# A fused attention and SoLU kernel: the second parts of its weights made by products with unit matrices, its chunks taken from two batches by turns, all steps in a new order

## The chip, the cores and the metric

The kernel runs on one core of one Trainium2 chip. The metric is device time in microseconds, the median of three runs. One execution was also recorded by the hardware profiler; times of single instructions are from that one.

## The reference

Attention over 4 batches, 8 heads, 768 positions and a head size of 64, in which a query sees the first `n_sink` keys and a window of the last `window` ones; then, per token, two matrix products with an exponential and a normalisation between them.

```python
scores = scale * np.matmul(q, k.transpose(0, 1, 3, 2))
keep = is_sink | in_window                     # n_sink = 4, window = 128
scores = np.where(keep, scores, -1000000000.0)
a = softmax(scores); attn_out = np.matmul(a, v)
x = attn_out.transpose(0, 2, 1, 3).reshape(3072, 512)
h = x @ w_in                                   # 512 x 1024, held as 64-bit floats
solu = h * softmax(h)
ln = (solu - mean) / np.sqrt(var + 1e-06) * g_ln
out = ln @ w_out                               # 1024 x 512, held as 64-bit floats
```

## The kernel before

The 3072 tokens are 24 chunks of 128 (`n`), six to a batch (`NC`). A chunk needs its own 128 keys, the 128 before them in its batch, and the sinks. Every large product is made in two parts: a tile is split into its value rounded to the matmul type (`xh`, `w1h`, `w2h`, `uh`) and the rest (`xl`, `w1l`, `w2l`, `ul`), and three products with fp32r operands stand for one exact one.

One chunk goes through these steps, each a small function:

- `load_*` bring q, k and v; `turn_q`, `turn_k` transpose them on TensorE (L486); `take_*` and `rest_*` split them (L511, L517, L534, L539); keys go to a ring of four slots (`ring`), with the sinks copied beside each (`ring_sinks`); `swap_q` swaps halves of the queries by DMA (`qX`).
- `score` (L565, L566) makes 128 x 264 scores per head, `pick` and `mask` (L572, L583) choose and mask, `exps` (L593), `invert` and `normalise` (L604 on GpSimd) finish the softmax.
- `turn_p` (L611), `p_hi`, `p_lo` (L621) and `part_new`, `part_old` (GpSimd) make the transposed weights in two parts; `value` (L680 to L685) multiplies with this chunk's and the last chunk's values (`vs`) and the sinks' (`vsink`, L471 to L477); `gather` (L693), `shift` (DMA `ysh`) and `tokens` give `xt`; `x_hi`, `x_lo` split it.
- `hidden` (L731) makes `h`, 24 products of 512 columns into the only `h` buffer (two PSUM banks); `highest` and `peak` (L738, L743: `mx`, `nm`) wait for it; `solu_exp`, `solu` (L748, L753), `centre`, `square`; `turn_u` (L785), `u_hi`, `u_lo` (L789, L793); `project` (L800), 24 products into `o`; `scale`, `store`.

Chunk 0 is "native": its scores (L563) and values (L673) are plain fp32 products without splitting, since nothing else uses TensorE yet.

The weights come as 64-bit floats in 16 blocks of 128 x 512: blocks 0 to 7 are `w_in`, 8 to 15 are `w_out`. For each block, ScalarE takes the magnitude of the high words (`size_w`, L389), VectorE clamps it (`least_w`, L396), shifts it into the place of an fp32 number (`move_w`, L400), puts the sign in (`sign_w`, L404) and the top bits of the low words (`rest_w`, L409). `gain_w` (L416, ScalarE) multiplies `w_out` blocks by `g_ln`; `w_hi` (L423, ScalarE) rounds; `w_lo` (L428) subtracts, on VectorE for blocks 1, 3, 5 and 7 and on GpSimd for the others.

Each engine runs its instructions in the order of the program, which is set by hand: `PLAN`, `PLAN_W`, `FIRST` and `OWN` give every step of every chunk and block a number, and the steps are called in the order of these numbers. The numbers are sort keys, not times.

Of the kernel before, what the change touches and what calls it, by code (L numbers as in the profile page):

```python
# [10 lines left out]
F32 = mybir.dt.float32  # L11
# [9 lines left out]
    "load_k": (-47.23,),  # L21
    "load_q": (-49.03,),
    "load_v": (-40.42,),
    "turn_q": (-40.51,),
    "turn_k": (-37.07,),
    "take_q": (-40.3, -40.3),
    "rest_q": (-38.64, -38.21),
    "swap_q": (-37.8, -35.74),
    "keep_k": (-2.79,),
    "take_k": (-36.17, -35.65),  # L30
    "rest_k": (-34.67, -34.63),
    "ring_sinks": (-37.2,),
# [12 lines left out]
    "sinks_lo": (-17.35, -15.21),
    "v_hi": (-29.23, -19.54),
    "v_lo": (-19.05, -9.81),
    "sink_values": (-2.64,),
    "turn_sinks": (-13.45,),
    "take_sinks": (-11.96,),  # L50
    "value": (-7.08, -10.1, -4.27, -1.3),
    "gather": (-5.52, -8.67, -2.61, 0.37),
    "shift": (-3.46, 2.91),
    "tokens": (-1.59, 5.21),
    "x_hi": (-0.2, 5.51),
    "x_lo": (-0.09, 8.07),
    "hidden": (5.97, 7.49, 10.82, 12.58, 7.4, 10.94, 11.18, 12.62),
    "highest": (15.14, 15.95),
    "peak": (16.22,),
    "solu_exp": (17.91,),  # L60
    "solu": (19.52,),
    "centre": (21.83,),
    "square": (29.39,),
    "variance": (32.89,),
# [935 lines left out]
```

## Time and profile before

| | before |
|---|---|
| median of 3 runs | 529.26 us (528.01 to 530.07) |
| the profiled execution, whole | 532.71 us |
| its span, first to last instruction | 530.9 us |
| mean granted TensorE clock | 0.983 |
| ScalarE, GpSimd busy | 355.0 us (67%), 325.8 us (61%) |
| HBM read, written | 27.53 MB, 6.42 MB |

PE is TensorE's matmul, PEld its weight load, DVE is VectorE, ACT ScalarE, POOL GpSimd, SP the engine that issues all DMAs. A matmul row's own duration holds its way through the array; what a stream of them costs is the distance from one start to the next. A row of a group reads: line, engine, operation, output<-inputs, shapes, count, busy time in us, mean ns of one, and the idle time of the engine before them with what ended it.

### The profile page before, as it was taken

The numbers are of one execution on the slowest core, as the hardware profiler recorded it, in microseconds if no ns is written. First come the engines' busy times: TensorE is split into PE (matmuls) and PEld (weight loads), VectorE is DVE, ScalarE is ACT, GpSimd is POOL, SyncE is SP. The second block draws the span as 40 slices with busy tenths as digits, with TensorE's granted clock in tenths as the row PEclk, the third lists the DMA queues.
The fourth block names the chain that finished last, engine by engine and source line by source line (L and its number), as shares of the span: only waits on it lengthen the run. The fifth ranks groups of instructions, "written<-read, shape, count | busy, mean of one in ns | idle before, by whom it ended". The sixth has DMA issues, their size and how long they took to land.

```text
span 530.9 us, 9053 instructions
## 1 busy us (share of the span) xinstructions
PE 464.2 (87%) x2572; PEld 385.8 (73%) x2572; DVE 421.1 (79%) x1238; ACT 355.0 (67%) x945; POOL 325.8 (61%) x445
## 2 busy tenths in 40 slices
PE   0242776999989999999999999999999999999995
PEld 0131565878877888888888788787888878888874
DVE  3999879899968679888878997888789888777531
ACT  3674747768876476776776768577778767666442
POOL 1276427798864267677764658667854766677620
PEclk9999977899999999999999999999999999999999
DMA  6974332543532514533533543462654332320101
GB/s 239 303 163 99 99 62 51 108 102 79 137 86 61 128 31 120 130 71 104 113 87 78 120 103 74 103 156 52 135 138 94 75 93 70 79 73 15 56 31 44
DMA packets 103303, 52.57 MB, mean 99 GB/s; under 512 B 80400, under 2 KB 92176, under 8 KB 103248
## 3 DMA queue, kind: packets, MB, share of 16 engines
q1 hardware_dynamic: 103248, 51.93, 39.4%
q8 instruction: 23, 0.38, 0.3%
q14 instruction: 32, 0.26, 0.2%
HBM read 27.53 MB, written 6.42 MB: 64 GB/s over the span
## 4 chain that ended last, share of the span: by engine, by line
PE 60%; DVE 25%; DMA 4%; issue 4%; ACT 3%; POOL 3%; SPq 0%; DVEq 0%; POOLq 0%; ACTq 0%
PE o L800 18%; PE h L731 18%; PE s L565 4%; PE s L566 3%; DMA ysh<-y 3%; PE av L680 3%; PE utp L785 3%; DVE ring L539 3%; PE av L683 3%; PE ptp L611 2%; DVE qT L517 2%; DVE y L693 2%; DVE wbits L409 2%; DVE s L572 2%; DVE wbits L404 2%
## 5 line engine op out<-in xcount | busy, mean ns | idle before, releaser
L604 POOL TENSOR_TENSOR sc<-sc,rs 128x544 f32<-128x544 f32 (+1 forms) x48 | 52.7, 1097 | 76.1 <-DVE rs L599 64.0
L731 PE MATMUL h<-w1h,xh 128*128 128x512 f32 x192 | 82.3, 429 | 0.3 <-DVE u L753 0.3
L593 ACT ACTIVATE sc<-sc,nmx 128x136 f32<-128x136 f32 (+1 forms) x192 | 76.3, 401 | 8.1 <-DVE nmx L583 7.7
L800 PE MATMUL o<-w2h,uh 128*128 128x512 f32 x192 | 79.6, 415 | 0.0
L731 PE MATMUL h<-w1h,xl 128*128 128x512 f32 x192 | 76.7, 400 | 1.4 <-POOL xl L720 1.4
L565 PE MATMUL s<-ring,qT 128*128 128x264 f32 (+1 forms) x184 | 59.9, 327 | 19.6 <-DVE ring L539 9.5
L800 PE MATMUL o<-w2h,ul 128*128 128x512 f32 x192 | 76.3, 397 | 0.0
L731 PE MATMUL h<-w1l,xh 128*128 128x512 f32 x192 | 76.3, 397 | 0.0
L800 PE MATMUL o<-w2l,uh 128*128 128x512 f32 x192 | 75.7, 394 | 0.0
L693 DVE TENSOR_REDUCE y<-av 128x256 f32<-128x512 f32 x92 | 63.1, 687 | 9.6 <-POOL xl L720 5.2
L583 DVE CUSTOM_DVE_ANT_0 sc<-s,bias 128x136 f32<-128x136 f32 (+1 forms) x192 | 55.5, 295 | 13.4 <-PE s L566 6.9
L565 PEld LDWEIGHTS s<-ring,qT 128*128 128x128 f32 x184 | 36.9, 200 | 34.6 <-issue 15.4
L628 POOL TENSOR_SCALAR_AFFINE_SELECT pc<-pt 128x1024 fp32r<-128x1024 f32 x40 | 43.8, 1095 | 24.4 <-DVE pt L621 21.6
L566 PE MATMUL s<-ring,qX 128*128 128x264 f32 (+1 forms) x184 | 54.8, 300 | 1.7 <-DMA qX<-qT 1.7
L710 POOL TENSOR_TENSOR xt<-y,ysh 64x256 f32<-64x256 f32 x46 | 33.5, 729 | 35.7 <-DMA ysh<-y 29.7
L680 PE MATMUL av<-pc,vs 128*128 128x256 f32 x160 | 43.6, 294 | 3.3 <-DVE y L693 2.7
L793 DVE TENSOR_TENSOR ul<-utp,uh 128x512 fp32r<-128x512 f32 x48 | 33.0, 688 | 16.8 <-ACT uh L789 15.9
L731 PEld LDWEIGHTS h<-w1h,xl 128*128 128x128 f32 x192 | 36.6, 190 | 10.3 <-POOL xl L720 1.8
L634 POOL TENSOR_SCALAR_AFFINE_SELECT pt<-pt 128x1024 fp32r<-128x1024 f32 x40 | 43.7, 1092 | 0.4
L715 ACT CAST xh<-xt 128x256 fp32r<-128x256 f32 x46 | 18.7, 406 | 37.4 <-POOL xt L711 37.1
L800 PEld LDWEIGHTS o<-w2h,ul 128*128 128x128 f32 x192 | 36.1, 188 | 10.5 <-DVE ul L793 2.0
L683 PE MATMUL av<-pt,vs 128*128 128x256 f32 x160 | 42.4, 287 | 0.0
(132 smaller groups left out, 1294.2 us busy)
## 6 DMA issues: line engine op xcount, KB each, us to landing
qX<-qT SPq DMA_DIRECT2D x92, 128.0 KB, 2.3
kn<-in_k_dram SPq DMA_DIRECT2D x24, 256.0 KB, 4.0
qn<-in_q_dram SPq DMA_DIRECT2D x24, 256.0 KB, 3.6
vn<-in_v_dram SPq DMA_DIRECT2D x24, 256.0 KB, 3.2
out_dram<-ob SPq DMA_DIRECT2D x24, 256.0 KB, 2.4
ysh<-y SPq DMA_DIRECT2D x92, 64.0 KB, 2.1
wraw<-in_moe_w_in_dram SPq DMA_DIRECT2D x8, 512.0 KB, 6.9
wraw<-in_moe_w_out_dram SPq DMA_DIRECT2D x8, 512.0 KB, 6.4
```

Of the source, the lines that this page charges most:

```text
L565: nc.tensor.matmul(o, st["qT", n, x][:, r, :], rhs, start=True, stop=False)
L566: nc.tensor.matmul(o, st["qX", n, x][:, r, :], rhs, start=False, stop=True)
L583: nc.vector.tensor_tensor_reduce(out=st["sc", n, hb][:, j, c0:c1], in0=st["s", n, h].rearrange("p a x -> p (a x)")[:, c0:c1], in1=bias0 if ...
L593: nc.scalar.activation(sc[:, i, c0:c1], sc[:, i, c0:c1], AF.Exp, bias=nmx[:, i:i + 1], scale=-1.0, accum_out=ssum[:, i:i + 1])
L604: nc.gpsimd.tensor_tensor(sc[:, :, c0:c1], sc[:, :, c0:c1], rs.unsqueeze(2).to_broadcast([P, HB, c1 - c0]), op=ALU.mult)
L628: nc.gpsimd.affine_select(pc, pt.bitcast(F32), pattern=[[0, HB * 2], [1, P]], compare_op=ALU.is_ge, fill=0.0, base=0, channel_multiplier=-1)
L634: nc.gpsimd.affine_select(pt, pt.bitcast(F32), pattern=[[0, HB * 2], [-1, P]], compare_op=ALU.is_ge, fill=0.0, base=-1, channel_multiplier=1)
L680: nc.tensor.matmul(acc[:, x], lhs, pc[:, 2 * jp + x], start=(x == 0), stop=(alone and x == 1))
L683: nc.tensor.matmul(acc[:, x], lhs, pt[:, 2 * jp + x], start=False, stop=False)
L693: nc.vector.tensor_reduce(st["y", n, hb][:, jp], st["acc", n, pr].rearrange("p x s q -> p x q s"), axis=AX.X, op=ALU.add)
L731: nc.tensor.matmul(st["h", n][:, cols], a[:, kt % 2, :], w[:, kt, cols], start=(kt == 0 and m == 0), stop=(kt == KT1 - 1 and m == 2))
L800: nc.tensor.matmul(st["o", n], a[:, kt % 4, :], part(w, kt), start=(kt == 0 and m == 0), stop=(kt == KT2 - 1 and m == 2))
```

## The change

It has four parts.

1. **The weights' words.** `size_w` and `least_w` go. `lower_w` (ScalarE) scales the high words, read as fp32, by 2 to the -112, which puts the exponent where the shift needs it and keeps the sign; the masks of `move_w` and `sign_w` change with it, their number does not.
2. **The second parts.** `w_lo` is no subtraction any more. For each block, TensorE multiplies the fp32 block with a 128 x 128 diagonal of minus one (`dg_8`) or of minus `g_ln` (`dg_0` to `dg_7`, made by `gains`), in fp32, into PSUM (`sum_w`); adds the rounded part through the unit matrix in fp32r (`less_w`); and ScalarE takes the result out with the sign turned (`w_lo`). `w_in` blocks use the `h` buffer in PSUM for that, `w_out` blocks one of the two `tr` buffers that the transposes `ptp` and `utp` use. `gain_w` goes: `w_hi` multiplies by `g_ln` as it rounds. The diagonals take the two buffers of `xt`; `dg_8` keeps one until the last `w_in` block, so the others follow each other through the second.
3. **Two batches by turns.** `place` makes chunk n the chunk of batch 0 or 1 (later 2 or 3) by its parity, so that a chunk's predecessor is n - 2. Chunks 0 and 1 are both the first of a batch, and both are native. Each batch has two slots of the ring of its own, so the sinks are copied for the first two chunks of a batch only. `vs` has 8 buffers for 5, `vsink` and `vsraw` 2 for 1.
4. **The order.** All four tables of sort keys are new.

```diff
-    "load_k": (-47.23,),
...
+    "load_k": (-39.8,),
...
-    def size_w(_, j):
+    def lower_w(_, j):
         bits = st["wbits", j] = sb.tile([P, NB], I32, tag=BIT_TAGS[j], name=f"wbits_{j}", bufs=2 + (BIT_TAGS[j] != "ob"))
-        nc.scalar.activation(bits.bitcast(F32), raws[j][:, :, 1].bitcast(F32), AF.Abs)
-    def least_w(_, j):
-        t = st["wbits", j].bitcast(F32)
-        nc.vector.tensor_scalar(t, t, LEAST, MOST, op0=ALU.max, op1=ALU.min)
+        nc.scalar.activation(bits.bitcast(F32), raws[j][:, :, 1].bitcast(F32), AF.Copy, scale=2.0 ** -112)
...
-    def gain_w(_, j):
-        if j >= NW1:
-            kt = blocks[j][3]
-            nc.scalar.activation(st["w", j], st["w", j], AF.Copy, scale=g_sb[:, kt:kt + 1])
+    def gains(_, kt):
+        dg = st["dg", kt] = sb.tile([P, P], F32, tag="xt", name=f"dg_{kt}", bufs=2)
+        if kt < KT2:
+            nc.vector.tensor_scalar(dg, ident, g_sb[:, kt:kt + 1], -1.0, op0=ALU.mult, op1=ALU.mult)
+        else:
+            nc.scalar.mul(dg, ident, -1.0)
+    def sum_w(_, j):
+        if j < NW1:
+            t = st["ws", j] = ps_h.tile([P, NB], F32, tag="h", name=f"ws_{j}")
+        else:
+            t = st["ws", j] = ps_tr.tile([P, NB], F32, tag="tr", name=f"ws_{j}")
+        nc.tensor.matmul(t, st["dg", KT2 if j < NW1 else j - NW1], st["w", j], start=True, stop=False)
...
-        nc.scalar.copy(part(wh, kt, cols), st["w", j])
+        if j < NW1:
+            nc.scalar.copy(part(wh, kt, cols), st["w", j])
+        else:
+            nc.scalar.activation(part(wh, kt, cols), st["w", j], AF.Copy, scale=g_sb[:, kt:kt + 1])
+    def less_w(_, j):
+        wh, _, _, kt, cols = blocks[j]
+        nc.tensor.matmul(st["ws", j], ident_r, part(wh, kt, cols), start=False, stop=True)
     def w_lo(_, j):
-        eng = nc.vector if j in LO_DVE else nc.gpsimd
-        eng.tensor_tensor(part(wl, kt, cols), st["w", j], part(wh, kt, cols).bitcast(F32), op=ALU.subtract)
+        _, wl, _, kt, cols = blocks[j]
+        nc.scalar.mul(part(wl, kt, cols), st["ws", j], -1.0)
+    def place(n):
+        twos, i = divmod(n, 2 * NC)
+        return 2 * twos + i % 2, i // 2
...
-    slot_of = (0, 2, 1, 3)
+    def slot_of(n):
+        b, c = place(n)
+        return 2 * (c % 2) + b % 2
...
-        return n == 0
+        return n < 2
...
-        nc.gpsimd.tensor_copy(ring[:, :, slot, 0:4], st["ksink", b][:, :, a:a + 4].bitcast(F32))
+        if c < 2:
+            nc.gpsimd.tensor_copy(ring[:, :, slot, 0:4], st["ksink", b][:, :, a:a + 4].bitcast(F32))
```

What this does to the order is shown at three places.

The first matmuls of TensorE, before: `kt`, `qt` are transposes of chunk 0, `s_0_*` its scores.

```order
L486 MATMUL kt_0_184<-ident_89,kn_0_135 128x128 x4
L486 MATMUL qt_0_196<-ident_89,qn_0_140 128x128 x4
L563 MATMUL s_0_2_228<-kf_0_219,qf_0_226 128x128
L563 MATMUL s_0_3_246<-kf_0_219,qf_0_226 128x128
L563 MATMUL s_0_0_258<-kf_0_219,qf_0_226 128x128
L563 MATMUL s_0_4_260<-kf_0_219,qf_0_226 128x128
L563 MATMUL s_0_7_270<-kf_0_219,qf_0_226 128x128
L563 MATMUL s_0_1_278<-kf_0_219,qf_0_226 128x128
```

And now: `ws_5` is the PSUM tile of weight block 5, L420 its first product (`sum_w`), L434 the second (`less_w`).

```order
L420 MATMUL ws_5_170<-wbits_5_144,dg_8_152 128x512
L434 MATMUL ws_5_170<-w1h_62,ident_r_94 128x512
L505 MATMUL qt_0_191<-ident_89,qn_0_131 128x128 x4
L420 MATMUL ws_6_196<-wbits_6_148,dg_8_152 128x512
L420 MATMUL ws_9_198<-wbits_9_142,dg_1_187 128x512
L505 MATMUL kt_0_204<-ident_89,kn_0_138 128x128 x4
L434 MATMUL ws_6_196<-w1h_62,ident_r_94 128x512
L583 MATMUL s_0_3_235<-kf_0_232,qf_0_209 128x128
L583 MATMUL s_0_6_239<-kf_0_232,qf_0_209 128x128
L420 MATMUL ws_1_245<-wbits_1_146,dg_8_152 128x512
L434 MATMUL ws_1_245<-w1h_62,ident_r_94 128x512
```

Products of the weights now stand between the transposes and scores of chunk 0, from the first row on.

The first rows of VectorE on the weights, before: L396 is the clamp, L400 the shift, L404 the sign, L409 the low words.

```order
L396 TENSOR_SCALAR wbits_1_142<-wbits_1_142 128x512
L400 TENSOR_SCALAR wbits_1_142<-wbits_1_142 128x512
L404 SCALAR_TENSOR_TENSOR wbits_1_142<-wraw_1_119,wbits_1_142 128x512
L396 TENSOR_SCALAR wbits_10_144<-wbits_10_144 128x512
L409 SCALAR_TENSOR_TENSOR wbits_1_142<-wraw_1_119,wbits_1_142 128x512
L400 TENSOR_SCALAR wbits_10_144<-wbits_10_144 128x512
L396 TENSOR_SCALAR wbits_9_146<-wbits_9_146 128x512
L404 SCALAR_TENSOR_TENSOR wbits_10_144<-wraw_10_123,wbits_10_144 128x512
```

And now: L394 is the shift, L398 the sign, L403 the low words.

```order
L394 TENSOR_SCALAR wbits_9_142<-wbits_9_142 128x512
L394 TENSOR_SCALAR wbits_5_144<-wbits_5_144 128x512
L398 SCALAR_TENSOR_TENSOR wbits_9_142<-wraw_9_123,wbits_9_142 128x512
L394 TENSOR_SCALAR wbits_1_146<-wbits_1_146 128x512
L398 SCALAR_TENSOR_TENSOR wbits_1_146<-wraw_1_121,wbits_1_146 128x512
L398 SCALAR_TENSOR_TENSOR wbits_5_144<-wraw_5_119,wbits_5_144 128x512
L403 SCALAR_TENSOR_TENSOR wbits_9_142<-wraw_9_123,wbits_9_142 128x512
```

A block takes three rows of VectorE where it took four.

TensorE where chunk 1's `hidden` ends, before: `utp` are transposes of chunk 0's `u`, `o_0` its projection, `s_4` scores of chunk 4.

```order
L731 MATMUL h_1_895<-w1h_62,xl_1_1_927 128x512
L785 MATMUL utp_0_1_1021<-ident_89,u_0_837 128x128 x4
L565 MATMUL s_4_0_1033<-ring_118,qT_4_0_948 128x264
L566 MATMUL s_4_0_1033<-ring_118,qX_4_0_965 128x264
L800 MATMUL o_0_1036<-w2h_0_211,uh_0_0_961 128x512
L800 MATMUL o_0_1036<-w2l_0_212,uh_0_0_961 128x512
```

And now: `ws_14` and `ws_12` are the last two weight blocks, `av_2_3` a value tile of chunk 2.

```order
L751 MATMUL h_1_816<-w1h_62,xl_1_1_838 128x512
L420 MATMUL ws_14_936<-wbits_14_653,dg_6_873 128x512
L700 MATMUL av_2_3_957<-pc_2_1_777,vs_2_1_881 128x256
L703 MATMUL av_2_3_957<-pt_2_1_752,vs_0_1_542 128x256
L700 MATMUL av_2_3_957<-pc_2_1_777,vs_2_1_881 128x256
L703 MATMUL av_2_3_957<-pt_2_1_752,vs_0_1_542 128x256
L705 MATMUL av_2_3_957<-skt_2_876,vsink_0_801 128x2x128
L505 MATMUL qt_4_968<-ident_89,qn_4_864 128x128 x4
L820 MATMUL o_0_982<-w2h_0_201,uh_0_0_883 128x512
L820 MATMUL o_0_982<-w2l_0_202,uh_0_0_883 128x512
L820 MATMUL o_0_982<-w2h_0_201,ul_0_0_920 128x512
L420 MATMUL ws_12_986<-wbits_12_489,dg_4_747 128x512
```

Of the 16 blocks' products, 14 pairs stand ahead of this place and two behind it; chunk 2's values and chunk 4's transposes, which stood ahead of it, partly stand behind it.

More of the change, by code (lines that the diff above doesn't have):

```diff
@@ L49 @@
[L49 to L64, printed above, removed]
@@ L103 @@
[L103 to L107 removed]
+    "load_k": -31.55, "load_q": -20.55, "load_v": 1.19, "turn_q": 0.72, "turn_k": -0.61, "take_q": 1.24,
```

216 lines of the change are left out of this document (115 added, 101 removed), and 113 rows, old and new, of the table OWN.

## The prediction

> **What bounds the kernel now.** I read the page's busy shares first, then the table of windows, then the timelines of VectorE and TensorE at the places that the table points to, and last the groups by line, for the prices.
>
> The page's rows name PE as the busiest engine:
>
> ```profile
> span 530.9 us, 9053 instructions
> PE 464.2 (87%) x2572; PEld 385.8 (73%) x2572; DVE 421.1 (79%) x1238; ACT 355.0 (67%) x945; POOL 325.8 (61%) x445
> ```
>
> That share is a mean over two stages. In the table of windows the columns are the window, its length, busy us (and instructions) of PE, PEld, DVE, ACT and POOL, the granted clock, the DMA share and GB/s:
>
> ```profile
> 0.00:40.00 40.00, 9.53 (x36) 6.67 (x36) 30.32 (x77) 22.23 (x49) 15.44 (x34) 1.00 0.77 234
> 40.00:75.00 35.00, 18.39 (x67) 13.00 (x67) 30.47 (x84) 18.11 (x49) 15.19 (x15) 0.91 0.38 93
> 75.00:107.00 32.00, 27.37 (x151) 23.67 (x149) 27.85 (x80) 22.84 (x67) 22.95 (x27) 0.83 0.36 77
> 200.00:500.00 300.00, 295.91 (x1709) 249.67 (x1708) 247.64 (x748) 214.16 (x583) 203.54 (x276) 1.00 0.39 94
> 0.00:108.50 108.50, 56.61 (x260) 44.46 (x260) 90.11 (x242) 63.18 (x162) 54.97 (x79) 0.92 0.52 142
> ```
>
> From 200 to 500 us PE is idle for 4.1 us in 300: there nothing but less work on PE helps, and the change takes none away. In the first 107 us PE is busy for 9.53 + 18.39 + 27.37 = 55.3 us only, while VectorE is busy for 90.11 of 108.5: this start-up hangs on VectorE, and it is where the change can gain. Where it ends shows in VectorE's timeline (start, duration, engine, line):
>
> ```profile
> 106.95 0.68 DVE L738 TENSOR_REDUCE mx<-h 128x1 f32<-128x512 f32 x1
> ...
> 108.46 0.21 DVE L743 TENSOR_SCALAR nm<-mx 128x1 f32<-128x1 f32 x1
> ```
>
> This is chunk 1. Its `h` ends at 106.9, and from there PE has no more gaps that count. I split the span there: t1 = 106.9, and R = 530.9 - 106.9 = 424.0 for the rest.
>
> **The change, part by part.** First, what VectorE has less of ahead of chunk 1's `nm`. The counts are from the two orders, the prices from the groups by line (count, then busy us and mean ns of one, then the idle time ahead):
>
> ```profile
> L396 DVE TENSOR_SCALAR wbits<-wbits 128x512 f32<-128x512 f32 x16 | 9.0, 560 | 7.6 <-ACT wbits L389 7.6
> L428 DVE TENSOR_TENSOR w1l<-wbits,w1h 128x512 fp32r<-128x512 f32 x4 | 2.7, 677 | 0.0
> L517 DVE TENSOR_TENSOR qT<-qt,qT 64x512 fp32r<-64x512 f32 x46 | 31.6, 688 | 4.8 <-ACT qT L511 3.5
> L539 DVE TENSOR_TENSOR ring<-kt,ring 64x512 fp32r<-64x512 f32 x46 | 31.6, 688 | 4.7 <-ACT ring L534 2.3 <-PE h L731 1.4
> L572 DVE COPY_PREDICATED s<-m_cur,s 128x128 f32<-128x128 int32 x96 | 27.7, 292 | 18.4 <-PE s L566 17.9
> L621 DVE TENSOR_TENSOR pt<-ptp,pt 128x512 fp32r<-128x512 f32 x46 | 31.5, 685 | 1.5 <-ACT pt L615 1.1
> L693 DVE TENSOR_REDUCE y<-av 128x256 f32<-128x512 f32 x92 | 63.1, 687 | 9.6 <-POOL xl L720 5.2 <-PE av L685 2.8 <-PE av L680 0.7
> L793 DVE TENSOR_TENSOR ul<-utp,uh 128x512 fp32r<-128x512 f32 x48 | 33.0, 688 | 16.8 <-ACT uh L789 15.9
> L477 DVE TENSOR_TENSOR vsink<-vsx,mine 128x512 fp32r<-128x512 f32 x4 | 3.7, 934 | 0.1
> L303 DVE TENSOR_SCALAR bias<-scratch_f 128x128 f32<-128x128 f32 x3 | 0.6, 224 | 0.1
> L720 DVE TENSOR_TENSOR xl<-xp,xh 128x256 fp32r<-128x256 f32 x2 | 0.8, 420 | 0.0
> L530 DVE COPY kf<-kt 128x512 f32<-128x512 f32 x1 | 0.7, 679 | 0.0
> ```
>
> Gone or moved behind: 16 clamps x 0.560 = 9.0; 4 `w_lo` x 0.677 = 2.7; 4 `rest_q` and 4 `rest_k` x 0.688 = 5.5; 9 picks x 0.292 = 2.6; 3 `p_lo` x 0.685 = 2.1; 5 `gather` x 0.687 = 3.4. Together 25.3. Of these only the clamps and `w_lo`, 11.7, are gone; the other 13.6 are chunk 2's to 4's work, which was ahead of chunk 1's end and now stands behind it or, with chunk 1 native, is not needed. Added: 8 diagonals, at the 128 x 128 row's 0.224, 1.8; one more `u_lo` 0.69; a second set of sink values about 1.9 (its product is the 0.934 row, two smaller steps come with it); one more `kf` 0.68 and two more `xl` 0.42, together 1.5. Sum 5.9. Net 25.3 - 5.9 = 19.4, so `nm` at 108.46 - 19.4 = 89.1, and t1 = 87.5 as `h` ends 1.5 ahead of `nm`. This keeps VectorE's 18.4 us of idle time as it is.
>
> Second, what PE has more of. Its rows, of single instructions first (the first row is a run of eight), then of groups:
>
> ```profile
> 10.45 0.68 DVE L409 SCALAR_TENSOR_TENSOR wbits<-wraw,wbits 128x512 int32<-128x512 int32 x1
> ```
> ```profile
> 28.65 2.41 PE L563 MATMUL s<-kf,qf 64*128 64x128 f32 x8 [4.03 <-DVE nmx L583]
> ...
> 72.35 0.63 PE L731 MATMUL h<-w1l,xh 128*128 128x512 f32 x1
> 72.77 0.63 PE L731 MATMUL h<-w1h,xl 128*128 128x512 f32 x1
> ...
> 76.46 0.39 PE L731 MATMUL h<-w1l,xh 128*128 128x512 f32 x1
> 76.69 0.40 PE L731 MATMUL h<-w1h,xl 128*128 128x512 f32 x1
> ...
> 95.76 0.61 PE L731 MATMUL h<-w1h,xh 128*128 128x512 f32 x1
> 96.19 0.42 PE L731 MATMUL h<-w1l,xh 128*128 128x512 f32 x1
> ...
> 96.67 0.28 PE L565 MATMUL s<-ring,qT 128*128 128x264 f32 x1
> 96.79 0.29 PE L566 MATMUL s<-ring,qX 128*128 128x264 f32 x1
> ```
> ```profile
> L563 PE MATMUL s<-kf,qf 64*128 64x128 f32 x16 | 4.2, 476 | 6.1 <-DVE nmx L583 4.4 <-DVE kf L530 1.8
> L673 PE MATMUL xp<-pt,vn 128*64 128x128 f32 x16 | 2.8, 447 | 1.5 <-ACT pt L615 1.5
> L565 PE MATMUL s<-ring,qT 128*128 128x264 f32 (+1 forms) x184 | 59.9, 327 | 19.6 <-DVE ring L539 9.5 <-DVE nmx L583 5.7 <-ACT sk L643 1.6
> L680 PE MATMUL av<-pc,vs 128*128 128x256 f32 x160 | 43.6, 294 | 3.3 <-DVE y L693 2.7 <-ACT skt L662 0.6
> L611 PE MATMUL ptp<-ident,sc 128*128 128x128 f32 x192 | 31.0, 287 | 3.2 <-POOL sc L604 2.3 <-DVE nm L743 0.6 <-DVE pt L621 0.3
> ```
>
> `less_w` is an fp32r product of 512 columns: 0.43 from start to start at 72 us, 0.23 at 76. I take 0.43. `sum_w` is plain fp32 with 512 columns, which before has nowhere. Its nearest rows are the native scores, fp32 with 128 columns: eight in 2.41 us, 0.301 each, so 4 x 0.301 = 1.2 for 512 columns. Its bounds are 0.23, if fp32 cost no more than fp32r, and 4 x 0.476 = 1.90 by the mean of one native score. I take 1.2, by the run of eight, since a distance is what a stream costs. 14 pairs stand ahead of chunk 1's end: 14 x (1.2 + 0.43) = 22.8 (14 x 0.46 = 6.4 to 14 x 2.33 = 32.6). The other counts there: 8 transposes x 0.287, 16 wide scores x 0.32 and 30 value products x 0.294 fewer, 16.2; 8 native scores x 0.476 and 8 native values x 0.447 more, 7.4; net -8.8. PE's busy time in the start-up goes from 55.3 by +14.0 to 69.3 (52.9 to 79.1).
>
> What time is that? The products can begin when the first block's low words are in, 10.45 + 0.68, about 11; with rounding 12. PE's densest start-up window, 75 to 107, has it busy for 27.37 of 32, a share of 0.86. At that share t1 = 12 + 69.3 / 0.86 = 92.6 (73.5 to 104). By PE's price alone it is thus a close second to VectorE's 87.5, and each waits for the other in turns; I put t1 at 90, between the two.
>
> A rule speaks against the change's price here. The Trainium skill, page "FP8 and Floating Point Precision", section "TensorE Precision Notes", says that true fp32 takes four passes through the array. By it and the cold 0.43 one `sum_w` would take 1.72 where the run of eight gives 1.2, an estimate, and t1 would be 12 + 76.6 / 0.86 = 101, the median about 531. The rows hold 2.41 / (8 x 128) = 2.35 ns a column for fp32 with 64 rows of weights, against 0.43 / 512 = 0.83 for cold fp32r, a factor of 2.8.
>
> Third, what moves behind t1. 22 value products and 16 wide scores for 16 narrow ones, 8 transposes, two pairs of weight products: the warm distance of 256 or 264 columns is 0.12 (96.67 to 96.79), so 22 x 0.12 = 2.6, 16 x 0.06 = 1.0, 8 x 0.06 = 0.5, and 2 x (1.2 + 0.23) = 2.9; together 7.0. The last two products hold both `tr` buffers until ScalarE's `w_lo` has emptied them, behind chunk 1's exponential, so the transposes of chunk 3's softmax may wait for 0 to 2 us; I take 1. The rest is 424.0 + 8.0 = 432.
>
> Now the other engines, whose rows are these:
>
> ```profile
> L789 ACT CAST uh<-utp 128x512 fp32r<-128x512 f32 x48 | 28.0, 583 | 17.7 <-PE utp L785 15.6 <-POOL xt L710 1.7 <-POOL w2l L428 0.2
> L428 POOL TENSOR_TENSOR w1l<-wbits,w1h 128x512 fp32r<-128x512 f32 x4 | 5.2, 1308 | 9.6 <-ACT w1h L423 9.6
> ```
>
> ScalarE reads 512 columns from PSUM in 0.583, so 14 `w_lo` bring 8.2, about what the 8 `gain_w` and the attention steps that move behind take off; it is busy for 63.18 of 108.5, and a balance of +1 or +2 lies in its 45 us of idle time. Were that cover gone, it would be 2 us. GpSimd loses its subtractions of 1.3 us each, 8 of them on `w_out`. The batches by turns and the fewer copies of sinks cost and bring nothing from 200 to 500 us, where PE's 4.1 us of idle time are all that could go. Loads move the same bytes by SP's queue in another order, and the 234 GB/s of the first 40 us fall to 93 behind them, so the weights are in by then either way; I cost it at 0.
>
> **The sum.** t1 = 90, rest 432, span 522. The profiled execution lies 532.71 - 530.9 = 1.8 over its span: 523.8. It was itself 532.71 - 529.26 = 3.45 over the median of the three runs, so I forecast a median of 520.4. No change is t1 = 98.9. I call 0.5% (2.6 us) what a measurement of this kernel can tell from no change: faster is below 526.6, t1 under 96.2; slower is above 531.9, t1 over 101.5.
>
> **The rivals.**
>
> *Products of the weights become the bound of the start-up (slower).* If a `sum_w` costs 1.90, as the mean row L563 says, PE has 79.1 us of work ahead of chunk 1's end, and t1 = 12 + 79.1 / 0.86 = 104: span 536, median 534. It decides from 1.75 for one `sum_w`: 14 x (1.75 + 0.43) - 8.8 = 21.7, 77.0 busy, t1 = 101.5. For it: 2.8 times the price of fp32r by column in the native rows, and weights of 128 rows where these had 64. Against it: the run of eight at 0.301.
>
> *One buffer for the `w_in` blocks (no change).* Each of the eight holds the only `h` buffer from `sum_w` to `w_lo`, and its diagonal keeps one of the two `xt` buffers, so the other diagonals follow each other through the second. Blocks 1, 3, 5 and 7 before waited long for rounding: the L428 row of GpSimd shows 9.6 us idle for four blocks. If a block holds `h` for 7.5 us (a `sum_w` and `less_w` of 1.6, the two ScalarE steps of 0.6, and 4.7 of waiting in two queues, twice that 2.4), then chunk 0's `hidden` cannot begin before 12 + 60 = 72, as it began before the change, and chunk 1's end comes 26 to 30 behind: t1 97 to 102, median 527 to 532. For it: the order puts most of those products far apart. Against it: the first two blocks' pairs stand among the very first rows of PE.
>
> *Denser products wake the clock (faster still).* The start-up's 512-column distance is 0.43 at 72 us, 0.23 at 76 and 0.43 again at 95.8, and the granted clock is 0.91 and 0.83. If the added products keep PE at 0.23, `sum_w` is 0.65 and PE stops counting; VectorE's idle time, much of it behind PE (17.9 us of L572's 18.4 over the run), shrinks by 10 of its 18.4: `nm` at 79, t1 = 77.5, median 508. The Trainium skill, page "TensorE: Matmul & The Clock Gate", Part 1, has half the clock as the default and the full one after about 3.4 us of activity; the distances at 72, 76 and 95.8 us agree.
>
> **How the numbers follow.** Forecast 0.60, denser products 0.12, the single buffer 0.10, products as the bound 0.18. Of both signs, but the forecast's own range, t1 from 86 to 94 (median 516 to 524), holds over half. Faster takes the forecast and the denser products, 0.72; the same is the single buffer, 0.10; slower 0.18. The low end takes in half of the densest case, t1 = 75.6 or median 506; the high end reaches 531, t1 = 100.6, and holds the single buffer but not the price of 1.90.
>
> **What would show it.** In the changed kernel's trace: chunk 1's first `mx` row at about 90 us; the rows of `sum_w` with a distance to the next start near 1.2 us; PE busy for about 69 us ahead of that `mx`, VectorE for 71 to 73; about 432 us from there to the end, with PE still idle for 4 us in a 300 us window of the middle. A `mx` row past 99 with `sum_w` at 1.8 or more shows the first rival; past 97 with long waits of `sum_w` for `w_lo` the second; below 80 with distances of 0.23 the third. The prediction is wrong in its split if the rest is under 426 or over 438 whatever t1 is: then the order of the middle or the end, which I costed at 8 us, did it.

## The result, and the profile after

The changed kernel takes 506.61 us (median of 4 runs, 503.57 to 508.99), the kernel before 528.79 (528.01 to 530.07). The ratio is 0.9575, with a 95% interval of 0.9519 to 0.9632: 22.2 us faster, where 8.9 were forecast. The direction was right; the gain was two and a half times the forecast.

The page of the changed kernel, then its windows (busy us of PE, PEld, DVE, ACT and POOL, granted clock, DMA share, GB/s), then the row of VectorE that ends the start-up:

```profile
span 504.3 us, 9115 instructions
PE 467.7 (93%) x2628; PEld 384.3 (76%) x2628; DVE 400.0 (79%) x1219; ACT 351.0 (70%) x953; POOL 305.0 (60%) x413
```
```profile
0.00:40.00 40.00, 20.95 (x76) 11.68 (x77) 28.03 (x87) 24.76 (x55) 9.26 (x20) 0.96 0.87 255
40.00:75.00 35.00, 31.25 (x157) 20.76 (x156) 30.94 (x102) 30.91 (x86) 19.00 (x31) 0.95 0.36 84
...
200.00:500.00 300.00, 295.10 (x1700) 251.49 (x1698) 239.05 (x716) 206.85 (x562) 192.40 (x255) 1.00 0.35 85
0.00:79.76 79.76, 56.96 (x262) 36.63 (x263) 62.72 (x204) 59.42 (x155) 31.79 (x54) 0.96 0.62 170
```
```profile
79.76 1.29 DVE L758 TENSOR_REDUCE mx<-h 128x1 f32<-128x512 f32 x2
82.16 0.20 DVE L763 TENSOR_SCALAR nm<-mx 128x1 f32<-128x1 f32 x1
```

Chunk 1's `mx` starts at 79.8 us (before 106.95, forecast 90), and what follows takes 504.3 - 79.8 = 424.5 (before 424.0, forecast 432). In these two profiles the whole gain shows as a shorter start-up (the profile of before is 3.9 us above its median, that of the change 0.5 below), and both terms of the sum came out lower than forecast, by 10 and by 7.5. PE's busy time ahead of `mx` is 57.0 us, almost the 55.3 of before, where 69.3 were forecast; VectorE's fell from 88.6 to 62.7, where 71 to 73 were forecast.

Why is VectorE's time lower? In rows of the weights' words whose shapes the change leaves alone, first of the kernel before, then of the changed one with the row of its diagonals last (count, busy us and mean ns, idle time ahead):

```profile
L400 DVE TENSOR_SCALAR wbits<-wbits 128x512 int32<-128x512 int32 x16 | 7.7, 488 | 0.1
L404 DVE SCALAR_TENSOR_TENSOR wbits<-wraw,wbits 128x512 int32<-128x512 int32 x16 | 11.2, 717 | 0.1
L409 DVE SCALAR_TENSOR_TENSOR wbits<-wraw,wbits 128x512 int32<-128x512 int32 x16 | 13.3, 846 | 0.1
```
```profile
L394 DVE TENSOR_SCALAR wbits<-wbits 128x512 int32<-128x512 int32 x16 | 6.6, 420 | 8.6 <-ACT wbits L390 8.4
L398 DVE SCALAR_TENSOR_TENSOR wbits<-wraw,wbits 128x512 int32<-128x512 int32 x16 | 10.8, 683 | 0.1
L403 DVE SCALAR_TENSOR_TENSOR wbits<-wraw,wbits 128x512 int32<-128x512 int32 x16 | 11.5, 731 | 0.1
L411 DVE TENSOR_SCALAR dg<-ident,g_sb 128x128 f32<-128x128 f32 x8 | 3.4, 429 | 0.5 <-PE ws L420 0.5
```

The same three operations on the same shapes are shorter by 68, 34 and 115 ns in the mean. The means hide a few very long rows. The timelines of VectorE and of GpSimd in the kernel before, at three places, show where those stand:

```profile
18.64 1.49 DVE L396 TENSOR_SCALAR wbits<-wbits 128x512 f32<-128x512 f32 x1
20.05 1.49 DVE L400 TENSOR_SCALAR wbits<-wbits 128x512 int32<-128x512 int32 x1
...
28.31 0.28 DVE L583 CUSTOM_DVE_ANT_0 sc<-s,bias 128x128 f32<-128x128 f32 x1
...
62.59 1.27 DVE L473 SCALAR_TENSOR_TENSOR vsx<-vsink,sign,vsx 128x64 f32<-128x64 f32 x1
```
```profile
18.52 1.33 POOL L428 TENSOR_TENSOR w1l<-wbits,w1h 128x512 fp32r<-128x512 f32 x1 [8.95 <-ACT w1h L423]
19.81 1.44 POOL L428 TENSOR_TENSOR w2l<-wbits,w2h 128x512 fp32r<-128x512 f32 x1
...
27.92 1.59 POOL L428 TENSOR_TENSOR w2l<-wbits,w2h 128x512 fp32r<-128x512 f32 x1 [6.66 <-DMA wraw<-in_moe_w_in_dram]
...
62.50 1.28 POOL L428 TENSOR_TENSOR w2l<-wbits,w2h 128x512 fp32r<-128x512 f32 x1
```

A row of VectorE of 64 columns or more that reads only SBUF (the memory that the engines share; PSUM is the one that TensorE writes to) and starts while GpSimd subtracts does not end before GpSimd's row does: the shift that takes 0.42 alone starts at 20.05 and ends at 21.54, GpSimd's row at 19.81 + 1.44 = 21.25. The first row of the sinks' values has 64 columns and lasts 1.27 us beside GpSimd's 1.28. A row that reads PSUM is not held: the one at 28.31 reads the scores `s` and takes its 0.28 while GpSimd subtracts from 27.92 to 29.51. In the kernel before, six rows of VectorE start during a subtraction and are held; together they last 6.2 us longer than the shortest rows of their kinds.

PE shows a second thing. Four transposes, in the kernel before and in the changed one, and the first products of the changed one (start, duration):

```profile
16.88 1.09 PE L486 MATMUL kt<-ident,kn 128*128 128x128 f32 x4 [16.88 <-DMA kn<-in_k_dram]
```
```profile
15.10 2.04 PE L420 MATMUL ws<-wbits,dg 128*128 128x512 f32 x2 [15.10 <-DVE wbits L403]
16.16 1.42 PE L434 MATMUL ws<-w1h,ident_r 128*128 128x512 f32 x1
17.37 1.05 PE L505 MATMUL qt<-ident,qn 128*128 128x128 f32 x4
...
20.63 0.60 PE L505 MATMUL kt<-ident,kn 128*128 128x128 f32 x4
...
34.25 1.02 PE L420 MATMUL ws<-wbits,dg 128*128 128x512 f32 x2
35.21 0.48 PE L583 MATMUL s<-kf,qf 64*128 64x128 f32 x2
```

Four transposes take 1.09 us before, and 0.60 in the changed kernel from 20.6 us on, with products between them. One `sum_w` (the trace keeps two rows of it) and its `less_w` take 17.37 - 15.10 = 2.27 at the first place, of which 0.43 is `less_w`: 1.84; at 34.25 a `sum_w` takes 0.96.

### The profile page after: what moved, and what is told of

It is laid out like the page before. It is cut to its first block, busy times and chain, and to the rows that moved or that the text cites. A ratio compares the mean times of both kernels' runs of the same rounds, so it can differ in the third digit from the quotient of the medians.

```text
span 504.3 us, 9115 instructions
## 1 busy us (share of the span) xinstructions
PE 467.7 (93%) x2628; PEld 384.3 (76%) x2628; DVE 400.0 (79%) x1219; ACT 351.0 (70%) x953; POOL 305.0 (60%) x413
## 4 chain that ended last, share of the span: by engine, by line
PE 67%; DVE 18%; ACT 7%; issue 4%; DMA 3%; SPq 1%; DVEq 0%; ACTq 0%
PE o L820 20%; PE h L751 20%; PE s L585 4%; PE utp L805 3%; PE s L586 3%; PE av L703 3%; PE av L700 3%; PE ptp L631 3%; DVE ring L558 2%; DVE y L713 2%; PE kt L505 2%; DMA wraw<-in_moe_w_in_dram 2%; DVE mx L758 2%; DVE sc L603 2%; ACT ring L553 2%
## 5 line engine op out<-in xcount | busy, mean ns | idle before, releaser
L751 PE MATMUL h<-w1h,xh 128*128 128x512 f32 x192 | 79.6, 414 | 0.1
L713 DVE TENSOR_REDUCE y<-av 128x256 f32<-128x512 f32 x88 | 60.3, 687 | 12.3 <-PE av L705 11.3
L585 PE MATMUL s<-ring,qT 128*128 128x264 f32 (+1 forms) x176 | 54.5, 317 | 4.5 <-DVE nmx L603 2.4
L648 POOL TENSOR_SCALAR_AFFINE_SELECT pc<-pt 128x1024 fp32r<-128x1024 f32 x40 | 43.8, 1094 | 21.8 <-DVE pt L641 15.3
L635 ACT CAST pt<-ptp 128x512 fp32r<-128x512 f32 x44 | 25.6, 583 | 42.7 <-PE ptp L631 42.5
L586 PE MATMUL s<-ring,qX 128*128 128x264 f32 (+1 forms) x176 | 48.8, 284 | 1.6 <-DMA qX<-qT 1.6
L553 ACT CAST ring<-kt 64x512 fp32r<-64x512 f32 x44 | 25.6, 581 | 32.0 <-PE kt L505 16.0
L558 DVE TENSOR_TENSOR ring<-kt,ring 64x512 fp32r<-64x512 f32 x44 | 30.3, 688 | 21.4 <-ACT ring L553 21.0
L585 PEld LDWEIGHTS s<-ring,qT 128*128 128x128 f32 x176 | 33.3, 189 | 15.3 <-issue 7.1
L740 POOL TENSOR_TENSOR xl<-xt,xh 128x256 fp32r<-128x256 f32 x44 | 32.5, 738 | 19.0 <-ACT xh L735 18.8
```

The source lines that it names most:

```text
L558: eng.tensor_tensor(t[ROWS[1 - x]], src[ROWS[x]], t[ROWS[x]].bitcast(F32), op=ALU.subtract)
L585: nc.tensor.matmul(o, st["qT", n, x][:, r, :], rhs, start=True, stop=False)
L586: nc.tensor.matmul(o, st["qX", n, x][:, r, :], rhs, start=False, stop=True)
L648: nc.gpsimd.affine_select(pc, pt.bitcast(F32), pattern=[[0, HB * 2], [1, P]], compare_op=ALU.is_ge, fill=0.0, base=0, channel_multiplier=-1)
L713: nc.vector.tensor_reduce(st["y", n, hb][:, jp], st["acc", n, pr].rearrange("p x s q -> p x q s"), axis=AX.X, op=ALU.add)
L751: nc.tensor.matmul(st["h", n][:, cols], a[:, kt % 2, :], w[:, kt, cols], start=(kt == 0 and m == 0), stop=(kt == KT1 - 1 and m == 2))
```

## The experiments

Medians are of 4 or 5 runs each; differences are from the changed kernel's 506.61 where nothing else is said, and ratios are to the kernel before, measured beside each run (527.7 to 529.1).

**Is PE full in the start-up?** Every `sum_w` issued twice.

```diff
+        nc.tensor.matmul(t, st["dg", KT2 if j < NW1 else j - NW1], st["w", j], start=True, stop=True)
         nc.tensor.matmul(t, st["dg", KT2 if j < NW1 else j - NW1], st["w", j], start=True, stop=False)
```

> The changed kernel with every sum_w issued twice; the second overwrites the first in PSUM. Theory V (VectorE sets the end of the start-up, PE has slack ahead of it): in the changed kernel's trace a sum_w takes about 0.9 us of PE, so PE gets about 14 x 0.9 = 12.6 us more work ahead of chunk 1's mx, of which its 22.8 us of idle time there take in all but 0 to 4; mx at 80 to 84 where it stood at 79.8, median 507 to 511. Rival P (PE's products set it): mx at about 92, median 519.

Measured: 514.53 us, ratio 0.973 (0.9696 to 0.9764), +7.9. The window up to chunk 1's `mx`:

```profile
0.00:87.81 87.81, 68.92 (x290) 41.86 (x291) 61.86 (x205) 59.94 (x155) 30.19 (x54) 0.96 0.57 155
```

Neither theory's number. PE's busy time grew by 12.0 and `mx` moved by 8.1: PE has some slack, but only a third of what is added goes into it. Theory V in its strict form falls.

**Is VectorE?** One clamp per block back, ahead of the shift.

```diff
+        f = t.bitcast(F32)
+        nc.vector.tensor_scalar(f, f, -3.0e38, 3.0e38, op0=ALU.max, op1=ALU.min)
         nc.vector.tensor_scalar(t, t, 3, 0x7FFFFFF8, ...
```

> The changed kernel with one clamp of 128 x 512 per weight block put back on VectorE ahead of the shift. Theory V: 16 x 0.42 to 0.56 us, 6.7 to 9.0, nearly all of it on the path: chunk 1's mx at 86 to 88, median 513 to 515. Rival P (PE's products set the start-up): mx within 2 us of 79.8, median 507 to 509.

Measured: 514.02 us, ratio 0.9725 (0.9694 to 0.9757), +7.4.

```profile
0.00:88.31 88.31, 60.62 (x262) 38.16 (x263) 70.64 (x220) 59.69 (x155) 29.78 (x54) 0.90 0.56 154
```

VectorE's busy time grew by 7.9, `mx` moved by 8.6: as theory V says. Together with the run before it: in the changed start-up added work on either engine moves the end. That this is because a block goes from one to the other is argued.

**Does GpSimd slow VectorE?** Twelve subtractions on GpSimd, unused.

```diff
+    def beside(j):
+        st["both", j] = st.get(("both", j), 0) + 1
+        if st["both", j] == 2 and j not in (1, 3, 5, 7):
+            wh, _, _, kt, cols = blocks[j]
+            nc.gpsimd.tensor_tensor(st["w", j], st["w", j], part(wh, kt, cols).bitcast(F32), op=ALU.subtract)
```

It is called at the end of `sum_w` and of `w_hi`.

> The changed kernel with 12 subtractions of 128 x 512 put back on GpSimd (blocks other than 1, 3, 5, 7), whose results nobody uses; the products stay. Theory V with sharing (VectorE's rows get longer while GpSimd subtracts): the means of move_w, sign_w, rest_w go from 420, 683, 731 ns towards the 488, 717, 846 of before, 16 x 0.22 = 3.5 us in all, mx at 82 to 85 and the median 509 to 512. Rival (GpSimd does not matter, rows got shorter because of the order): the three means stay within 15 ns, and mx within 1 us.

Measured: 516.91 us, ratio 0.9801 (0.9744 to 0.9858), +10.3, where 2 to 5 were expected. The profiled execution, 514.6, is the fastest of four that reach 520.4; against the profile of the change it is 8.5 longer. The window, then one pair of rows on VectorE and GpSimd:

```profile
0.00:85.68 85.68, 58.99 (x262) 37.27 (x263) 69.64 (x204) 59.48 (x155) 45.04 (x63) 0.94 0.58 159
...
41.10 1.77 DVE L403 SCALAR_TENSOR_TENSOR wbits<-wraw,wbits 128x512 int32<-128x512 int32 x1
```
```profile
40.83 1.49 POOL L419 TENSOR_TENSOR wbits<-wbits,w1h 128x512 f32<-128x512 f32 x1 [1.82 <-PE ws L426]
```

VectorE executes the same 204 rows, and they take 69.6 us instead of 62.7. The three means go to 498, 683 and 925 ns from 420, 683 and 731; in the sum 4.4 us against the 3.5 expected. `mx` comes 5.9 later, and another 2.6 are lost behind it. The kernel has no use for what GpSimd computes, and it is 10 us slower. One part of this is not separated: the subtraction also holds the words' buffer longer (ScalarE's `lower_w` waits for GpSimd once, 2.0 us).

**The change without its products.** The new order and the scaled words, with the second parts by subtraction.

```diff
-        nc.tensor.matmul(t, st["dg", KT2 if j < NW1 else j - NW1], st["w", j], start=True, stop=False)
+        beside(j)
...
+            eng = nc.vector if j in (1, 3, 5, 7) else nc.gpsimd
+            eng.tensor_tensor(part(wl, kt, cols), st["w", j], part(wh, kt, cols).bitcast(F32), op=ALU.subtract)
```

> The changed kernel's order, scaled words and batches by turns, but the second parts by subtraction again: on VectorE for blocks 1, 3, 5, 7, on GpSimd for the others, with the gain multiplied in by ScalarE; no diagonals, no sum_w, no less_w, no w_lo on ScalarE. Theory V: VectorE gets 4 x 0.68 = 2.7 back, 3.5 from longer rows, and loses 3.4 of diagonals, so mx moves by +1 to +5 and the median is 508 to 512. Rival P (the products cost more than they bring): mx earlier by 5 or more, median 501 or less. Rival O (the order alone made the gain): mx within 1 us.

Measured: 521.89 us, ratio 0.9878 (0.9847 to 0.9909), +15.3, three times what theory V allowed; rival P and rival O fall.

```profile
0.00:89.24 89.24, 48.43 (x221) 35.85 (x222) 70.23 (x201) 56.98 (x146) 44.09 (x63) 0.98 0.56 153
```

So the products bring 15.3 us, and all else in the change 528.0 - 521.9 = 6.1 against the kernel before that was measured beside this run (6.9 against 528.8). Between the two profiles 9.5 of the loss lie ahead of chunk 1's `mx`, and 4.6 behind it, where the granted clock is 0.50 from 98.6 to 105.3 us; in the change it is full there.

**The scaled words alone**, in the kernel before.

```diff
-        nc.scalar.activation(bits.bitcast(F32), raws[j][:, :, 1].bitcast(F32), AF.Abs)
+        nc.scalar.activation(bits.bitcast(F32), raws[j][:, :, 1].bitcast(F32), AF.Copy, scale=2.0 ** -112)
...
-        nc.vector.tensor_scalar(t, t, LEAST, MOST, op0=ALU.max, op1=ALU.min)
```

> The kernel before, in its own order, with the words scaled instead of clamped: ScalarE scales by 2 to the -112, the 16 clamps on VectorE are gone, the two masks change; all else as before. Theory V (VectorE's work sets the end of the start-up): chunk 1's mx earlier by 7 to 9 us, at 98 to 100, median 519 to 522. Rival (the order of before holds other waits in the start-up): mx earlier by less than 4 us, median 525 or more.

Measured: 523.20 us, ratio 0.9911 (0.9883 to 0.9939), 4.7 us less than the kernel before; `mx` comes at 100.6, 6.3 earlier, where 7 to 9 were expected. VectorE's busy time ahead of `mx` fell by 6.4 (88.6 to 82.2), not by the 9.0 of the clamps' rows: the clamps that stood beside GpSimd, up to 1.49 us long, are gone, but other rows now stand there (the shift's mean goes from 488 to 528 ns).

**Turns, sort keys or sinks: the middle.** Three kernels, each undoing one: batches 2 and 3 one after the other; the two tables of before for chunks 5 to 21; sinks copied for each chunk.

```diff
-        twos, i = divmod(n, 2 * NC)
-        return 2 * twos + i % 2, i // 2
+        if n >= 2 * NC:
+            return divmod(n, NC)
+        return n % 2, n // 2
```
```diff
-        return round(16 * n + PLAN[name][i] + (FIRST.get(name, 0) if place(n)[1] == 0 else 0), 2)
+        plan, first = (PLAN_B, FIRST_B) if 5 <= n <= 21 else (PLAN, FIRST)
+        return round(16 * n + plan[name][i] + (first.get(name, 0) if place(n)[1] == 0 else 0), 2)
```
```diff
-        if c < 2:
+        if c < NC:
```

> The changed kernel with batches 2 and 3 (chunks 12 to 23) one after the other, chunk n - 1 as predecessor, sinks copied for four chunks of each; chunks 0 to 11 and all sort keys as in the change. Theory T (turns give the middle its 7.8 us): the time from nm of chunk 12 to nm of chunk 22, 179.2 us in the change, gets longer by 3 us or more, median 509 to 512. Theory O (the sort keys give it): it stays within 1.5 us, median 505 to 508.

> The changed kernel with the sort keys of before (the table by step and the offsets of a batch's first chunk) for chunks 5 to 21; all else as in the change, turns included. Theory O (the sort keys give the middle its 7.8 us): nm of chunk 2 to nm of chunk 23, 379.7 us in the change, goes to 384 to 390, median 511 to 516. Theory T (turns give it): within 2 us of 379.7, median 505 to 509.

> The changed kernel with the sinks copied beside every chunk's keys as before, 24 copies on GpSimd instead of 8; the copied values are the same. Theory S (fewer copies free GpSimd and VectorE): nm of chunk 2 to nm of chunk 23 grows from 379.7 by 3 us or more, median 510 or more. Theories O and T: within 1.5 us, median 505 to 508.

Measured: 509.81 (ratio 0.965, 0.9602 to 0.9698), 534.67 (1.0122, 1.0086 to 1.0157) and 506.21 (0.9574, 0.9531 to 0.9617). The rows of `nm` of chunk 2 and chunk 23, of the kernel before, of the run with scaled words alone, of the change, and of these three:

```profile
125.92 0.21 DVE L743 TENSOR_SCALAR nm<-mx 128x1 f32<-128x1 f32 x1
...
513.36 0.21 DVE L743 TENSOR_SCALAR nm<-mx 128x1 f32<-128x1 f32 x1
```
```profile
119.61 0.21 DVE L742 TENSOR_SCALAR nm<-mx 128x1 f32<-128x1 f32 x1
...
503.97 0.21 DVE L742 TENSOR_SCALAR nm<-mx 128x1 f32<-128x1 f32 x1
```
```profile
106.19 0.21 DVE L763 TENSOR_SCALAR nm<-mx 128x1 f32<-128x1 f32 x1
...
485.86 0.21 DVE L763 TENSOR_SCALAR nm<-mx 128x1 f32<-128x1 f32 x1
```
```profile
106.17 0.21 DVE L766 TENSOR_SCALAR nm<-mx 128x1 f32<-128x1 f32 x1
...
489.17 0.21 DVE L766 TENSOR_SCALAR nm<-mx 128x1 f32<-128x1 f32 x1
```
```profile
109.86 0.21 DVE L826 TENSOR_SCALAR nm<-mx 128x1 f32<-128x1 f32 x1
...
515.73 0.21 DVE L826 TENSOR_SCALAR nm<-mx 128x1 f32<-128x1 f32 x1
```
```profile
109.30 0.21 DVE L763 TENSOR_SCALAR nm<-mx 128x1 f32<-128x1 f32 x1
...
489.30 0.21 DVE L763 TENSOR_SCALAR nm<-mx 128x1 f32<-128x1 f32 x1
```

The stretch is 387.4 us before, 384.4 with the words scaled (same steps in the middle), 379.7 in the change, 383.0 with half the batches one by one, 405.9 with the old keys, 380.0 with the sinks copied for each chunk. So of the 7.8 us between the two profiles 3.1 lie between two executions of the same middle, and 4.7 are the change's. A third profile with the old middle (the kernel before with added products, below) has 385.0; nine other profiles with the change's turns and keys have 378.9 to 380.0. The gain does not lie in the second half: from chunk 12 to 22 the kernel before takes 179.6 (178.4 with the words scaled), the change 179.2. Turns bring 3.3 us for the kernel as it stands, though not where theory T put it: from chunk 12 to 22 it is only 1.6 us (180.8 against 179.2), 1.7 come earlier. The sinks bring nothing. The old keys with the new turns are slower than either kernel, so theory O can't be read from that run.

**Is it the clock?** The run that subtracts again, with `sum_w` and `less_w` issued as well, read by nobody.

```diff
     def sum_w(_, j):
+        nc.tensor.matmul(t, ident, st["w", j], start=True, stop=False)
         beside(j)
...
+        nc.tensor.matmul(st["ws", j], ident_r, part(wh, kt, cols), start=False, stop=True)
```

> The changed order with subtraction on VectorE and GpSimd as in the run that subtracts again, and with sum_w and less_w issued beside it, with plain unit matrices, at their places and into their PSUM tiles, but read by nobody: some 28 us of PE rows that give nothing. In the run that subtracts again the granted full clock begins at 65 us, in the changed kernel at 18.6. Theory C (the products wake the clock, and that is worth more than they cost): full clock from 18 to 25 us on, mx of chunk 1 at 84 to 88 instead of 89.2, median 516 to 521. Rival W (the products only cost PE's time and buffers): mx at 92 to 97, median 525 to 530.

Measured: 519.34 us, ratio 0.9837 (0.9796 to 0.9879), 2.5 less than without them.

```profile
0.00:87.87 87.87, 62.05 (x261) 38.28 (x261) 71.71 (x200) 57.00 (x146) 44.77 (x63) 0.90 0.56 155
```

PE is busy for 13.6 us more and `mx` comes 1.4 earlier: products that give nothing cost nothing here. The trace's record of the granted clock has its first full stretch at 20.9 us, where it stood at 64.4 without them, and falls back to half from 24.3 to 37.9. Time and `mx` are where theory C put them, but the 2.5 us are not clear of the noise: the intervals of the two ratios overlap. Nor are they the worth of the clock by itself, which stands in them against the time that the added products take.

And products of the unit matrix with itself in the kernel before:

```diff
     def w_hi(_, j):
+        if ("h", 0) not in st:
+            t = ps_h.tile([P, NB], F32, tag="h", name=f"warm_{j}")
+            for _ in range(2):
+                nc.tensor.matmul(t, ident, ident.unsqueeze(1).to_broadcast([P, 4, P]), start=True, stop=True)
```

> The kernel before with two products of the unit matrix with itself, fp32, 512 columns, issued at each w_hi ahead of chunk 0's hidden (12 places, into the h buffer, read by nobody): 12 x 2 x 0.9 to 1.8 us of PE work, 22 to 43, into 51.6 us of PE's idle time. Theory C: the clock wakes at 15 to 25 us where it was 65, and mx of chunk 1 comes 2 to 6 us earlier than 105 to 107, median 522 to 526. Rival W: mx later by 3 us or more, median 531 or more. If the clock falls asleep again between the places, nothing is told.

Measured: 533.84 us against 529.08, ratio 1.0109 (1.0069 to 1.0149): slower by 4.8, the time of rival W, though `mx` comes only 1.9 later (108.9). But the clock did not stay awake: it is full from 7.0 us on, and half again from 10.4 to 24.0, 34.3 to 37.7, 44.5 to 54.8, 71.8 to 78.7 and 88.9 to 95.7. By the condition that was set beforehand this run tells nothing of what an early clock is worth in the old order; it tells that these products cost 4.8.

**Can more be taken off VectorE?** Its eight diagonals on ScalarE.

```diff
-            nc.vector.tensor_scalar(dg, ident, g_sb[:, kt:kt + 1], -1.0, op0=ALU.mult, op1=ALU.mult)
+            nc.scalar.activation(dg, ident, AF.Copy, scale=g_neg[:, kt:kt + 1])
```

> The changed kernel with its eight diagonals of minus g_ln made on ScalarE (scaled by a column of minus g_ln) instead of VectorE. Theory V (VectorE's work counts one to one in the start-up): VectorE loses 8 x 0.43 = 3.4 us, mx of chunk 1 earlier by 2 to 3.4 us at the same granted clock, median 503 to 505. Rival (the ends of the start-up are PE and ScalarE by now, and ScalarE gets 8 x 0.3 us): median 506 to 509.

Measured: 506.41 us, ratio 0.9574 (0.9541 to 0.9607): no difference from the change that shows, as the rival has it. The four runs of the change spread over 5.4 us, so a gain of 2 or 3 is not excluded by the medians.

```profile
0.00:81.25 81.25, 58.96 (x262) 37.63 (x263) 60.66 (x196) 61.36 (x164) 30.61 (x54) 0.94 0.60 167
```

VectorE has 2.1 us less to do ahead of `mx`, ScalarE 1.9 more, and in the profile `mx` comes 1.5 later, with the clock at 0.94 for 0.96. More work on VectorE costs; that less of it pays is not seen.

**Which subtractions were dear?** Two halves of the run that subtracts again: only VectorE's four, or (with `j in`) only GpSimd's twelve.

```diff
+    def by_product(j):
+        return j not in (1, 3, 5, 7)
```

> The changed kernel with the second parts of blocks 1, 3, 5 and 7 subtracted on VectorE again; the other twelve by products. All second parts by subtraction cost 15.3 us (521.9 against 506.6). Theory G (GpSimd's twelve subtractions are most of that): VectorE gets 4 x 0.68 = 2.7, PE loses four pairs, 4.5; median 505 to 510. Rival H (the four on VectorE are most of it): 514 to 519.

> The converse: blocks 1, 3, 5 and 7 by products, the other twelve subtracted on GpSimd again, the gain of w_out by ScalarE as before, no diagonals of g_ln on VectorE (3.4 us less there). Theory G: 12 us of GpSimd rows that VectorE's rows wait for, and the clock woken late; median 515 to 521. Rival H: 505 to 510.

Measured: 512.52 (ratio 0.9706, 0.9682 to 0.973), +5.9, and 517.99 (0.9808, 0.978 to 0.9835), +11.4. The windows up to `mx` with the four, then with the twelve:

```profile
0.00:87.05 87.05, 59.96 (x250) 38.52 (x251) 65.26 (x209) 57.65 (x151) 29.75 (x54) 0.86 0.57 156
```
```profile
0.00:89.82 89.82, 57.24 (x233) 39.58 (x234) 66.47 (x196) 59.14 (x151) 43.89 (x63) 0.92 0.55 152
```

Theory G gets the twelve right and the four too low (rival H has those at 514 to 519): 5.9 and 11.4 make 17.3, about the 15.3 of all sixteen. The four give VectorE only 2.5 us more work but move `mx` by 7.3. With four pairs of products fewer, PE's busy time does not fall (60.0 against 57.0) and the clock shows 0.86 for 0.96: PE has gaps where those pairs stood first, and runs slower after them. That this is the cause is argued from these two columns, not tried. With the twelve, too, not all is in VectorE's rows: `mx` comes 10.1 later, of which VectorE's busy time is 3.8 (3.4 of diagonals are saved in it) and its idle time 6.3, and the clock's first full stretch begins at 54.5 us, where the change has it at 18.6.

## Why the prediction was wrong in size

Right were the sign, the start-up as the place of the gain, VectorE as an engine to count there, and the count for all but the products. Without the products the prediction's own sum gives VectorE 25.3 - 2.7 less and 5.9 - 1.8 more, so `nm` at 108.46 - 18.5 = 90.0 and `h` done at 88.5; the run that subtracts again has `mx` at 89.2. VectorE's idle time there is 89.2 - 70.2 = 19.0, for 18.4 before: the assumption that it stays held there and in the change (79.8 - 62.7 = 17.0), though not in every run (23.4 with the twelve subtractions alone).

The step that failed is a clause in the part on the other engines: "GpSimd loses its subtractions of 1.3 us each", with those of VectorE's `w_lo` costed at their own 2.7 us, and the products added on PE as a pure cost. As a term, "products for subtractions" stood in the sum as about 1 us of VectorE's time gained and 2.5 lost to PE in the mean of 87.5 and 92.6. It measured 15.3 us of time.

- GpSimd's twelve, costed at nothing, are worth 11.4 us where they replace products, and 10.3 where they are added unread. VectorE's rows wait for GpSimd's, and the price list of the prediction was taken from rows in which that waiting is contained. Of VectorE's 6.5 us beyond the forecast, the words' three steps make 16 x (0.068 + 0.034 + 0.115) = 3.5, and the sinks' values 3.6 (two sets were costed at 4.1 + 1.9, and the changed kernel's take 1.2 each), two smaller rows 1.1; the diagonals cost 1.6 more than costed (0.429 for 0.224, one of them 1.29 long beside GpSimd). Not all of the waiting was behind subtractions: two of the words' long rows stand beside GpSimd's splitting of the values (L459). The sign was in the profile: a shift of 0.42 alone and 1.49 at 20.05 us.
- The price of `sum_w`, 1.2, lies between what it is at full clock, 0.96, and at half, 1.84. The four passes that the Trainium skill gives for true fp32 (page "FP8 and Floating Point Precision", section "TensorE Precision Notes") agree with the rows: 0.96 is 4.2 times the 0.23 of an fp32r product, 1.84 is 4.3 times 0.43. The estimate of 531 us worked out from it did not come about, since most products met the full clock.
- PE's busy time was forecast to grow by 14.0 and grew by 1.7. The products came, but the rows beside them got shorter: four transposes 0.60 for 1.09. The third rival had this mechanism, its 508 us is near the result, and its sign came: `mx` below 80, with distances of 0.23 among the products. Yet its sum is not what happened: VectorE's idle time was to shrink by 10 us and shrank by 1.4, where its busy time shrank by 6.5 more than forecast. The low end of the stated range, 506, was set by this rival; that the time falls just inside it is luck. What the early clock is worth by itself no run separates.
- The first rival, PE as the bound, is half true: PE's work does count in the changed start-up (7.9 us for sums issued twice), but it is far from making the kernel slower. The second, the single buffer, did not show: chunk 0's `mx` came at 65.5 instead of 83.1.
- The rest was forecast at 432 and took 424.5, under the 426 below which the prediction called its own split wrong. The 7.0 us of work that moves there, and the wait, are to be seen: `nm` of chunk 1 to `nm` of chunk 2 goes from 17.5 to 24.0. Some 3 us of the miss are in the 424.0 that it started from: two other profiles with the same steps there, the words scaled and the products added, have 420.6 and 421.0. What was missed besides is the middle, costed at nothing because PE had 4.1 us of idle time in 300: 4.7 us of the change. A PE that shows 98.6% busy is not one that cannot become faster: from chunk 2's `nm` to chunk 23's it executes 2175 instructions in both kernels, and is busy with them for 374.8 us in the change, 380.0 before and 378.8 with the words scaled.

What stays open: how the 4.7 us of the middle divide between turns and keys, and how much of the 11.4 us is VectorE's longer rows, how much the longer hold of the words' buffers, and how much the clock that wakes later.

## What to carry to other kernels

Before an engine's small steps are costed at nothing because it is "off the path", look for rows of the bounding engine that are far above their own minimum, and see what the other engine does at that moment: the minimum of a row, not its mean, is what it costs alone, and here most of the difference belonged to the neighbour. Where a start-up passes blocks from one engine to another, test the bound in both directions: here 7.9 us more on VectorE cost 7.4, 12.0 more on PE cost 7.9, and 2.1 less on VectorE brought nothing that shows. And work that fills a sparse PE is not priced by the rows of the sparse PE, since it changes their clock.

## What the runs showed of the hardware

- A row of VectorE on data in SBUF that starts during a two-input row of GpSimd lasts until that one ends, and then some: 1.49 for 0.42 us, and 1.27 for a row of 64 columns that takes 0.28 alone. So it is with all 20 such rows of 64 columns or more in the first 110 us of the kernel before and of the change. Rows that read PSUM are not held (0.28 inside GpSimd's 1.59), nor are some of one column (0.20 at 82.16 in the change, inside GpSimd's 0.73 from 81.69).
- The clock column shows 1.00 for the first 40 us of the kernel before, in which four transposes take 1.09 us, while in the changed kernel four take 0.60 at 20.6 us. It is no sign of full speed ahead of the first stretch that ran at it.
- The four runs of the changed kernel differ by 5.4 us (503.57 to 508.99), and their mean granted clocks are 0.993 and 0.982 at the two ends: 0.011 x 505 = 5.6 us of full clock. In the profile of the change the clock is half twice in the start-up, for 3.4 us each time (28.8 to 32.2 and 45.9 to 49.3); in that of the kernel which copies the sinks for each chunk the second stretch lasts 10.2 us (45.7 to 56.0), and `mx` comes 3.1 later, with VectorE busy for 62.1 us as against 62.7.
- A plain fp32 product of 128 x 128 with 512 columns takes 0.96 us at full clock and 1.84 at half, and leaves two rows in the trace (32 for the 16 blocks).
